# Linear attention into a SwiGLU block: k and v laid out with nine positions per partition and head pairs in two row halves, block 0's q with two tokens per partition, and one weight piece rounded earlier

## The chip, the cores and the metric

The kernel runs on one core of one Trainium2 chip. The metric is the device time of one execution in microseconds (us). Times in this document come from repeated executions and from one execution that was recorded by the hardware profiler; the profiled execution has its own time, which is given beside its span.

## What is computed

The reference is an attention without softmax, a norm, and then a gated feed-forward block, all in 32-bit floats:

```
q, k, v: (8 batches, 8 heads, 576 positions, 64)
kv  = einsum('bhsd,bhse->bhde', k, v)          # one 64x64 matrix per batch and head
out = einsum('bhsd,bhde->bhse', q, kv)
out = out / sqrt(mean(out*out, -1) + 1e-6) * g_norm
x   = out as (4608 tokens, 512)                # 8 heads x 64 side by side
y   = (silu(x @ w_gate) * (x @ w_val)) @ w_out # 512 -> 1536 -> 512
```

The weights are given as 64-bit floats. The kernel reads them as pairs of 32-bit words and rounds them to 32 bits itself.

## The kernel before, in words

**Blocks.** The 4608 tokens are cut into nine blocks of 512. A batch has 576 positions, so block n holds the end of batch n-1 and the start of batch n. `Att(n)` makes the normed attention output of block n, turned so that features lie on partitions (`self.x`), and `Ffn(n)` multiplies it with the weights. The attention of block n+1 is made inside the feed-forward work of block n. For block 0 nothing stands before it: `first` (L428) and `second` (L440) run at the start of the kernel.

**k and v.** `load_kv` (L215) loads, for a group g of four heads, two head pairs j = 2g and 2g+1. Of each pair, the lower 64 partitions hold the one part of the positions and the upper 64 the other: 5 positions per partition in one half and 4 in the other (5·64 + 4·64 = 576), so a load has runs of 1280 or 1024 bytes. That is four loads for k and four for v in each group, each onto 64 partitions. For block 0 v goes through ScalarE's queue (ACT's) and k through SyncE's (SP's). `kv` (L273) multiplies: each half of the rows accumulates into a PSUM tile of its own (`kv_ps[0]`, `kv_ps[1]`), ScalarE copies the first (L292), and VectorE adds the second to it (L293, helper line L111). Each of the 72 matmuls is 64x64: a quarter of the array[...].

**q.** `load_q` (L256) loads block 0's q as four loads of 128 tokens on 128 partitions, in runs of 64 values (256 bytes), and `turn_q` (L295) turns each 128 tokens by four 128x128 transposes on TensorE (L307), copied out by VectorE (the first) and ScalarE (the others). `product` (L313) multiplies with the 64x64 matrices, squares on ScalarE (L338) and sums on VectorE (L339). `root` (L341) finds 1/sqrt on VectorE in eleven small steps, `scale` (L359) applies it (helper line L113), `turn_x` (L366) turns the result on TensorE and multiplies by `g_norm` on ScalarE (L375).

**Weights.** `load_w` loads a piece of 512 KB (128 partitions, 1024-byte runs for gate and value pieces) into one of four `ld` buffers, which q also uses. `Words.round_to` (L138) rounds a piece: two ScalarE passes (L144 the low words, L146 the high words) and four on VectorE (L147, L152, L153, L157). The pieces go gate 0, value 0, gate 1, value 1 and so on; `plain_up` (L947) of output chunk f needs gate and value piece f.

**What orders the work.** The text is written in one order and a scheduler places each instruction on its engine's queue; each engine runs its queue in order. `tc.issue_after(x)` keeps what is inside it behind instruction x. Before the change the first two pieces (`weights(2)`) stand behind the squares and the scaling of block 0's first half. Loads take turns on a few semaphores, so an issue may also wait for an earlier load to land. In block 1's feed-forward, leaf weights for the later blocks are made on VectorE and stored to memory (`send`, L771); SP's queue holds these stores and the k and v loads of the next block in one line, and GpSimd (POOL) makes operand pieces (`t`, L112) in buffers that those stores have to release.

Of the kernel before, what the change touches and what calls it, by code (L numbers as in the profile page):

```python
# [8 lines left out]
F32 = mybir.dt.float32  # L9
# [5 lines left out]
P = 128  # L15
# [3 lines left out]
def kernel(  # L19
# [41 lines left out]
    nc = tc.nc  # L61
# [9 lines left out]
    NS = DM // P  # L71
    NF = FF // P
    NP = NF // 2
    KT = 5
    LD = 2 * (2 * KT - 1) * D
    eps = 1e-6
    assert NT == B * S and NT == NB * BLK and NB == B + 1 and S - BLK == BLK // B
    assert 2 * D == P and H == 2 * NS and (2 * KT - 1) * D == S and NS == 4

    def pool(name, bufs, **kw):  # L80
        return ctx.enter_context(tc.tile_pool(name=name, bufs=bufs, **kw))
# [37 lines left out]
    class Words:  # L119
# [18 lines left out]
        def round_to(self, dst):  # L138
            halves = self.raw.rearrange("p (f w) -> p f w", w=2)
            low, high = halves[:, :, 0], halves[:, :, 1]  # L140
            room = ring()

            unit = room[:, 0]
            nc.scalar.activation(out=unit, in_=low, func=ACT.Copy, scale=2.0**-51, bias=2.0)  # L144
            mag = room[:, 1].bitcast(U32)
            nc.scalar.activation(out=mag.bitcast(F32), in_=high.bitcast(F32), func=ACT.Abs)  # L146
            nc.vector.tensor_scalar(  # L147
                out=mag.bitcast(F32), in0=mag.bitcast(F32), scalar1=self.LOW, scalar2=self.HIGH,
                op0=OP.max, op1=OP.min,
            )  # L150
            sign = room[:, 2].bitcast(U32)
            nc.vector.tensor_scalar(out=sign, in0=high, scalar1=0x80000000, scalar2=None, op0=OP.bitwise_and)  # L152
            nc.vector.scalar_tensor_tensor(  # L153
                out=mag, in0=mag, scalar=3, in1=sign, op0=OP.logical_shift_left, op1=OP.bitwise_xor
            )
            a, b = self.shape[0], BLK // self.shape[0]
            nc.vector.tensor_tensor(  # L157
                out=dst.bitcast(U32),
                in0=mag.rearrange("p (a b) -> p a b", a=a, b=b),
                in1=unit.bitcast(U32).rearrange("p (a b) -> p a b", a=a, b=b),  # L160
                op=OP.add,
            )
# [22 lines left out]
    class Att:  # L185
# [28 lines left out]

        def load_kv(self, g):  # L215


            if self.n == B:
                return
            for i, (views, src) in enumerate(((self.k, k), (self.v, v))):  # L220
                tile_ = self.place_kv(g, i)
                for e in range(2):
                    j, s0 = 2 * g + e, 0
                    for r in range(2):
                        m = KT - (r != e)
                        at = 2 * D * (KT - r) * e
                        t = tile_[r * D : (r + 1) * D, at : at + 2 * D * m].rearrange("p (h x) -> p h x", h=2)
                        queue = nc.scalar if self.n == 0 and i else nc.sync
                        queue.dma_start(
                            out=t,  # L230
                            in_=src[self.n, 2 * j : 2 * j + 2, s0 : s0 + m * D].rearrange("h (p t) d -> p h (t d)", t=m),
                        )
                        views[j, r] = t.rearrange("p h (t d) -> p h t d", t=m)
                        s0 += m * D

        def load_quarters(self, i):

# [18 lines left out]
        def load_q(self, i):  # L256
            if self.n >= TURNED:
                self.load_quarters(i)
                return
            if self.n == 1:  # L260
                tiles = [t_tile().rearrange("p a b -> p (a b)") for _ in range(2)]
            else:
                ld = ld_pool.tile([P, LD], F32, name="ld")
                tiles = [ld[:, 0:BLK], ld[:, BLK : 2 * BLK]]
            for t in range(2):
                tile_ = tiles[t].rearrange("p (h d) -> p h d", h=H)
                for b, s0, p0, p1 in self.parts(2 * i + t):
                    nc.sync.dma_start(
                        out=tile_[p0:p1], in_=q[b, :, s0 : s0 + p1 - p0, :].rearrange("h p d -> p h d")
                    )  # L270
                self.q.append(tile_.rearrange("p (j u) d -> p j (u d)", u=2))

        def kv(self, g):  # L273


            if self.n == B:
                return
            if g == 0:
                self.kv_ps = [m_psum.tile([P, NS, D], F32, name="m") for _ in range(2)]
            for e in range(2):  # L280
                j = 2 * g + e
                for c in range(KT):
                    for r in range(2):
                        m = KT - (r != e)
                        for u in range(2 if c < m else 0):
                            nc.tensor.matmul(  # L286
                                self.kv_ps[r][u * D : (u + 1) * D, j, :], lhsT=self.k[j, r][:, u, c, :],
                                rhs=self.v[j, r][:, u, c, :], start=(c == 0), stop=(c == m - 1),
                            )
            if g == 1:  # L290
                dst = kvs[self.n % 3]
                nc.scalar.copy(out=dst, in_=self.kv_ps[0])  # L292
                self.kv_made = add(nc.vector, dst, self.kv_ps[1], dst)  # L293

        def turn_q(self, i, pools=None):  # L295

# [6 lines left out]
            for t in (2 * i, 2 * i + 1):  # L303
                pool = pools[t % 2] if pools else m_psum
                ps = pool.tile([P, NS, P], F32, name=pool.name[0])
                for j in range(NS):
                    nc.tensor.transpose(ps[:, j], self.q[t][:, j], ident)  # L307
                if t:
                    nc.scalar.copy(out=self.qt[:, t], in_=ps)
                else:  # L310
                    nc.vector.tensor_copy(out=self.qt[:, t], in_=ps)

        def product(self, i, pools=None):  # L313
# [7 lines left out]
            for t in range(2):  # L321
                for j in range(NS):
                    for b, _, p0, p1 in self.parts(2 * i + t):
                        for p in range(p0, p1, D):
                            for u in range(2):
                                rows = slice(u * D, (u + 1) * D)
                                nc.tensor.matmul(  # L327
                                    self.ps[i][u][p : p + D, t, j, :],
                                    lhsT=self.qt[rows, 2 * i + t, j, p : p + D], rhs=kvs[b % 3][rows, j, :],
                                    start=True, stop=True,  # L330
# [97 lines left out]
        def first(self):  # L428
            self.turn_q(0, (b_psum, c_psum))
            for g in range(2):  # L430
                self.kv(g)
            self.half(0)
            squared = self.squared
            self.turn_q(1, (b_psum, c_psum))
            with tc.issue_after(self.scaled.ins):
                self.product(1, (b_psum, a_psum))
            self.turn_x(0)
            return squared, self.scaled
# [437 lines left out]
    class Ffn:  # L876
# [3 lines left out]
            self.ps, self.making, self.leaf_room, self.ended = {}, [], None, None  # L880

        def store(self, o, t, columns=slice(None)):
            rows = out[BLK * self.n : BLK * (self.n + 1), columns].rearrange("(t p) d -> p t d", t=T)
            nc.sync.dma_start(out=rows[:, t : t + o.shape[1], :], in_=o)

        def h_sums(self, j, k, engine):

# [110 lines left out]
    blocks[0].load_q(0)  # L998
    for g in range(2):
        blocks[0].load_kv(g)  # L1000
    blocks[0].load_q(1)
    load_weights(4)
    squared, scaled = blocks[0].first()
# [89 lines left out]
```

## Time and profile before

| what | value |
|---|---|
| median of 5 runs | 1040.8 us (1039.66 to 1041.19) |
| profiled execution, its time | 1040.93 us |
| span of that execution in the trace | 1039.1 us, so 1.8 us lie around it |
| TensorE busy | 1009.7 us (97%) |
| VectorE, ScalarE, GpSimd busy | 700.3, 232.0, 368.9 us |
| mean granted TensorE clock | 0.997 |
| k loads in all (beside the start) | 26 of 160 KB and 26 of 128 KB, and as many for v |

The page gives the busy share of each engine, then the span in 40 slices, and then the chain of work that ended last: from the last instruction back to what released it, or to the instruction before it on its engine. A line of the chain, of the timeline and of a group names the source line (L286), the engine (PE is TensorE, PEld its weight loads, DVE VectorE, ACT ScalarE, SPq SyncE's queue) and the tile names, output first. "Issue" in the chain is time in which the engine waited for nothing that the profile shows. 32-bit matmuls appear as two records each, transposes as one.

### The profile page before, as it was taken

To read this page: it belongs to the slowest core of one execution; us is meant where nothing else is said; L and a number is where in the kernel's file an instruction comes from. 1 tells how busy PE (TensorE), PEld (TensorE's weight loads), DVE (VectorE), ACT (ScalarE), POOL (GpSimd) and SP (SyncE) were. 2 spreads that over 40 slices of the span, in tenths; PEclk is the share of its full clock that TensorE was granted. 3 is DMA by queue.
4 is the path that set the end of the run, shared out by engine and by line. 5 is a ranking of instruction groups with operands and counts; after the bars stand their busy time and mean duration, and the time that the engine had idled before them with its cause. 6 is when DMAs were issued, how large, how long until landed. Compare 5 with 4: busy or idle time off the path is not lost.

```text
span 1039.1 us, 21544 instructions
## 1 busy us (share of the span) xinstructions
PE 1009.7 (97%) x8588; PEld 906.2 (87%) x8588; DVE 700.3 (67%) x1202; ACT 232.0 (22%) x357; POOL 368.9 (35%) x280
## 2 busy tenths in 40 slices
PE   4899999899999999999999999999999999999998
PEld 3644688778899989998999899988999899989997
DVE  2999696788656866575666666684668566856661
ACT  3666111222212211211111111211122111212110
POOL 0000443435024621563147305640455136512670
PEclk9899999999999999999999999999999999999999
DMA  9588704765457556764676367736862666066611
GB/s 213 182 251 273 165 1 126 186 191 148 131 180 240 134 113 193 241 160 84 196 240 187 61 202 231 215 49 171 247 196 51 162 207 188 29 152 210 191 31 41
DMA packets 255044, 168.16 MB, mean 162 GB/s; under 512 B 124640, under 2 KB 230240, under 8 KB 254944
## 3 DMA queue, kind: packets, MB, share of 16 engines
q1 hardware_dynamic: 228384, 162.45, 55.8%
q10 hardware_dynamic: 26496, 4.33, 2.4%
q8 instruction: 68, 1.11, 0.4%
q14 instruction: 32, 0.26, 0.1%
q0 software_dynamic: 64, 0.00, 0.0%
HBM read 138.02 MB, written 22.41 MB: 154 GB/s over the span
## 4 chain that ended last, share of the span: by engine, by line
PE 89%; DVE 6%; DMA 3%; issue 1%; SPq 0%; POOL 0%; ACT 0%; DVEq 0%; POOLq 0%
PE b L662 25%; PE b L513 19%; PE c L662 12%; PE c L513 9%; PE a L662 6%; PE a L513 5%; PE b L956 4%; PE c L956 4%; PE m L286 1%; PE m L327 1%; DVE r L112 1%; DVE xi L112 1%; DVE r L111 1%; DMA h<-in_k_dram 1%; DVE t L111 1%
## 5 line engine op out<-in xcount | busy, mean ns | idle before, releaser
L111 POOL TENSOR_TENSOR r<-r 128x256 f32<-128x256 f32 (+1 forms) x105 | 110.8, 1061 | 309.1 <-DVE r L111 234.3
L111 DVE TENSOR_TENSOR r<-b,r 128x512 f32<-128x512 f32 (+1 forms) x273 | 162.0, 606 | 64.0 <-PE b L662 58.9
L112 POOL TENSOR_TENSOR t<-wo 128x512 f32<-128x512 f32 x81 | 115.3, 1447 | 195.5 <-DVE wo L111 107.8
L111 DVE TENSOR_TENSOR r<-c,r 128x512 f32<-128x512 f32 (+1 forms) x179 | 108.5, 618 | 89.1 <-PE c L662 49.5
L662 PE MATMUL b<-x,t 128*128 128x128 f32 x1092 | 151.0, 275 | 0.0
L662 PEld LDWEIGHTS b<-x,t 128*128 128x128 f32 x1092 | 136.5, 192 | 0.6
L111 DVE TENSOR_TENSOR r<-a,r 128x512 f32<-128x512 f32 (+1 forms) x99 | 62.5, 631 | 110.3 <-PE a L513 65.8
L113 POOL TENSOR_TENSOR h<-r 128x1024 f32<-128x1024 f32 (+1 forms) x40 | 81.6, 2057 | 87.3 <-DVE r L111 74.1
L662 PE MATMUL c<-xi,t 128*128 128x128 f32 x840 | 112.2, 275 | 0.3 <-DVE xi L111 0.3
L662 PEld LDWEIGHTS c<-xi,t 128*128 128x128 f32 x840 | 102.8, 192 | 0.4 <-DVE xi L111 0.4
L513 PE MATMUL b<-wo,h 128*128 128x256 f32 x432 | 99.4, 382 | 0.1
L513 PE MATMUL b<-t,h 128*128 128x256 f32 x432 | 96.9, 381 | 0.0
L513 PEld LDWEIGHTS b<-t,h 128*128 128x128 f32 x432 | 81.3, 190 | 11.3 <-issue 0.2
L513 PEld LDWEIGHTS b<-wo,h 128*128 128x128 f32 x432 | 79.9, 190 | 12.7 <-DVE h L113 2.5
L676 ACT COPY r<-b 128x512 f32<-128x512 f32 x63 | 36.9, 586 | 212.7 <-PE b L662 205.9
L662 PE MATMUL b<-xi,t 128*128 128x128 f32 x588 | 79.7, 276 | 0.0
L662 PEld LDWEIGHTS b<-xi,t 128*128 128x128 f32 x588 | 72.4, 192 | 0.0
L662 PE MATMUL b<-x,wg 128*128 128x128 f32 x336 | 52.7, 279 | 0.2 <-DVE x L112 0.2
L662 PE MATMUL b<-x,wv 128*128 128x128 f32 x336 | 51.3, 275 | 0.0
L956 PE MATMUL b<-x,wg 128*128 128x512 f32 (+1 forms) x112 | 45.8, 552 | 3.8 <-DVE wg L157 3.4
L513 PE MATMUL c<-t,s 128*128 128x256 f32 x216 | 48.3, 380 | 0.0
L513 PE MATMUL a<-wo,h 128*128 128x256 f32 x216 | 48.3, 379 | 0.0
(133 smaller groups left out, 1579.5 us busy)
## 6 DMA issues: line engine op xcount, KB each, us to landing
t<-w SPq DMA_DIRECT2D x336, 256.0 KB, 3.3
out_dram<-r SPq DMA_DIRECT2D x17, 512.0 KB, 3.1
ld<-in_moe_w_gate_dram SPq DMA_DIRECT2D x12, 512.0 KB, 4.6
ld<-in_moe_w_val_dram SPq DMA_DIRECT2D x12, 512.0 KB, 4.7
ld<-in_moe_w_out_dram SPq DMA_DIRECT2D x12, 512.0 KB, 5.1
w<-t SPq DMA_DIRECT2D x18, 256.0 KB, 2.5
w<-xi SPq DMA_DIRECT2D x12, 384.0 KB, 3.0
ld<-in_k_dram SPq DMA_DIRECT2D x26, 160.0 KB, 3.9
```

The source lines that it names most:

```text
L111: add = lambda e, o, a, b: e.tensor_tensor(out=o, in0=a, in1=b, op=OP.add)
L112: sub = lambda e, o, a, b: e.tensor_tensor(out=o, in0=a, in1=b, op=OP.subtract)
L113: mul = lambda e, o, a, b: e.tensor_tensor(out=o, in0=a, in1=b, op=OP.mult)
L286: nc.tensor.matmul(self.kv_ps[r][u * D : (u + 1) * D, j, :], lhsT=self.k[j, r][:, u, c, :], rhs=self.v[j, r][:, u, c, :], start=(c == 0), ...
L327: nc.tensor.matmul(self.ps[i][u][p : p + D, t, j, :], lhsT=self.qt[rows, 2 * i + t, j, p : p + D], rhs=kvs[b % 3][rows, j, :], start=True, ...
L513: nc.tensor.matmul(banks[e][:, e], lhsT=lhsT, rhs=rhs, start=first and i == 0 and (e == 0 or banks[0] is not banks[1]), stop=i == self.ste ...
L662: nc.tensor.matmul(ps[:, i, f], lhsT=self.weight(o, p, f), rhs=self.operand(o, p), start=first and (i, f) == (0, 0), stop=True, skip_group ...
L676: nc.scalar.copy(out=dst, in_=ps)
L956: nc.tensor.matmul(t, lhsT=w[f // 2][:, i, P * (f % 2) : P * (f % 2 + 1)], rhs=x[:, i, of], start=(i == 0), stop=(i == NS - 1),)
```

## The change

For every block, k and v are laid out with 9 positions per partition (`KT = 9`, runs of 2304 bytes): of the two head pairs in a group, the one lies wholly in the lower 64 partitions and the other wholly in the upper ones. A group then has two loads for k and two for v. k goes lower half first and v upper half first. No sum over the halves is left: each PSUM tile holds whole results for two head pairs, and is copied out by itself, in block 0 one on ScalarE and one on VectorE, in later blocks both on ScalarE.

Block 0's q is loaded as two loads of 256 tokens, two neighbouring tokens per partition (512-byte runs). It is turned by matmuls with the identity, one for each head (128 rows, 64 columns of the array) in place of transposes of head pairs: 16 matmuls for the 256 tokens where there were 8 transposes. Block 0's output rows are stored to fit.

The first gate piece is loaded between k's last load and q's second load, and is rounded behind the two copies of block 0's kv, ahead of the squares and sums of the first half. Turning q's second half now stands behind the product of the first half on TensorE. In rounding, ScalarE does the high words first.

```diff
-    KT = 5
-    LD = 2 * (2 * KT - 1) * D
+    KT = 9
+    LD = 2 * KT * D
...
             unit = room[:, 0]
-            nc.scalar.activation(out=unit, in_=low, func=ACT.Copy, scale=2.0**-51, bias=2.0)
             mag = room[:, 1].bitcast(U32)
             nc.scalar.activation(out=mag.bitcast(F32), in_=high.bitcast(F32), func=ACT.Abs)
+            nc.scalar.activation(out=unit, in_=low, func=ACT.Copy, scale=2.0**-51, bias=2.0)
...
                 tile_ = self.place_kv(g, i)
-                for e in range(2):
-                    j, s0 = 2 * g + e, 0
-                    for r in range(2):
-                        m = KT - (r != e)
-                        at = 2 * D * (KT - r) * e
-                        t = tile_[r * D : (r + 1) * D, at : at + 2 * D * m].rearrange("p (h x) -> p h x", h=2)
-                        queue = nc.scalar if self.n == 0 and i else nc.sync
-                        queue.dma_start(
-                            out=t,
-                            in_=src[self.n, 2 * j : 2 * j + 2, s0 : s0 + m * D].rearrange("h (p t) d -> p h (t d)", t=m),
-                        )
-                        views[j, r] = t.rearrange("p h (t d) -> p h t d", t=m)
-                        s0 += m * D
+                for r in (1, 0) if i else (0, 1):
+                    j = 2 * g + r
+                    t = tile_[r * D : (r + 1) * D].rearrange("p (h x) -> p h x", h=2)
+                    queue = nc.scalar if self.n == 0 and i else nc.sync
+                    queue.dma_start(
+                        out=t, in_=src[self.n, 2 * j : 2 * j + 2].rearrange("h (p t) d -> p h (t d)", t=KT)
+                    )
+                    views[j] = t.rearrange("p h (t d) -> p h t d", t=KT)
...
+            if self.n == 0:
+
+                ld = ld_pool.tile([P, LD], F32, name="ld")[:, 0 : 2 * BLK]
+                nc.sync.dma_start(
+                    out=ld.rearrange("p (h x) -> p h x", h=H),
+                    in_=q[0, :, HB * i : HB * (i + 1), :].rearrange("h (p t) d -> p h (t d)", t=2),
+                )
+                both = ld.rearrange("p (j u t d) -> p t j u d", j=NS, u=2, t=2)
+                self.q += [both[:, t] for t in range(2)]
+                return
...
-                self.kv_ps = [m_psum.tile([P, NS, D], F32, name="m") for _ in range(2)]
-            for e in range(2):
-                j = 2 * g + e
-                for c in range(KT):
-                    for r in range(2):
-                        m = KT - (r != e)
-                        for u in range(2 if c < m else 0):
-                            nc.tensor.matmul(
-                                self.kv_ps[r][u * D : (u + 1) * D, j, :], lhsT=self.k[j, r][:, u, c, :],
-                                rhs=self.v[j, r][:, u, c, :], start=(c == 0), stop=(c == m - 1),
-                            )
+                self.kv_ps = [m_psum.tile([P, 2, D], F32, name="m") for _ in range(2)]
+            for c in range(KT):
+                for r in range(2):
+                    k, v = self.k[2 * g + r], self.v[2 * g + r]
+                    for u in range(2):
+                        nc.tensor.matmul(
+                            self.kv_ps[r][u * D : (u + 1) * D, g, :], lhsT=k[:, u, c, :], rhs=v[:, u, c, :],
+                            start=(c == 0), stop=(c == KT - 1),
+                        )
             if g == 1:
-                dst = kvs[self.n % 3]
-                nc.scalar.copy(out=dst, in_=self.kv_ps[0])
-                self.kv_made = add(nc.vector, dst, self.kv_ps[1], dst)
+                dst = kvs[self.n % 3].rearrange("p (g r) d -> p r g d", r=2)
+                self.kv_made = [nc.scalar.copy(out=dst[:, 0], in_=self.kv_ps[0])]
+                if self.n:
+                    nc.scalar.copy(out=dst[:, 1], in_=self.kv_ps[1])
+                else:
+                    copied = nc.vector.tensor_copy(out=dst[:, 1], in_=self.kv_ps[1])
+                    self.kv_made.append(copied)
...
                 for j in range(NS):
-                    nc.tensor.transpose(ps[:, j], self.q[t][:, j], ident)
+                    if self.n:
+                        nc.tensor.transpose(ps[:, j], self.q[t][:, j], ident)
+                        continue
+                    for u in range(2):
+                        nc.tensor.matmul(ps[u * D : (u + 1) * D, j], lhsT=self.q[t][:, j, u], rhs=ident, start=True, stop=True)
...
-                                nc.tensor.matmul(
+                                self.multiplied = nc.tensor.matmul(
...
             for g in range(2):
                 self.kv(g)
+            with tc.issue_after(self.kv_made[0].ins), tc.issue_after(self.kv_made[1].ins):
+                weights(1)
             self.half(0)
             squared = self.squared
-            self.turn_q(1, (b_psum, c_psum))
+            with tc.issue_after(self.multiplied.ins):
+                self.turn_q(1, (b_psum, c_psum))
...
-            rows = out[BLK * self.n : BLK * (self.n + 1), columns].rearrange("(t p) d -> p t d", t=T)
-            nc.sync.dma_start(out=rows[:, t : t + o.shape[1], :], in_=o)
+            rows = out[BLK * self.n : BLK * (self.n + 1), columns]
+            if self.n:
+                rows = rows.rearrange("(t p) d -> p t d", t=T)[:, t : t + o.shape[1], :]
+            else:
+                rows = rows[P * t : P * t + HB].rearrange("(p t) d -> p t d", t=2)
+            nc.sync.dma_start(out=rows, in_=o)
...
     for g in range(2):
         blocks[0].load_kv(g)
+    load_weights(1)
     blocks[0].load_q(1)
```

## The prediction on record

> **What bounds the kernel now.** I read the page first, then the chain of waits by stretches, then the waits of TensorE, then the timelines of the stretches where the chain leaves TensorE. The page says that TensorE is nearly always busy:
>
> ```profile
> PE 1009.7 (97%) x8588; PEld 906.2 (87%) x8588; DVE 700.3 (67%) x1202; ACT 232.0 (22%) x357; POOL 368.9 (35%) x280
> ```
>
> So time can be won only where TensorE stands idle or runs slowly. From 245 us to the end its listed waits sum to 1.1 us, and between 40 and 245 us the only listed one is 6.6 us (4 times) for ScalarE's copies L563. The rest is the start. The chain there:
>
> ```profile
> 17.72 1.09 PE m L327 x63
> 18.80 0.94 issue
> ...
> 25.05 1.18 DVE z L339 x2
> ...
> 28.18 0.61 DVE wg L157
> 28.79 0.14 issue
> 28.93 3.75 PE b L956 x8
> 32.68 0.79 PE c L956 x4
> 33.47 1.17 issue
> 34.64 0.42 DVE h L113
> ...
> 37.01 0.61 DVE wg L157
> 37.62 0.04 issue
> 37.66 1.99 PE b L956 x8
> ```
>
> VectorE is to be seen as the limit from 20.67 to 28.79 and again from 34.64 to 37.62: norm of the first half, rounding of the first pieces, scaling of the second half, rounding of gate piece 1. From 37.66 to 116 us the chain is TensorE alone. I call T the end of kv (VectorE's L111, 17.15 + 0.42 = 17.57) and S the end of the first half's scaling (25.05).
>
> Stretches, with the TensorE clock as third figure from the right and GB/s as last:
>
> ```profile
> 5.00:7.90 2.90, 0.00 (x0) 0.00 (x0) 0.00 (x0) 0.00 (x0) 0.00 (x0) 1.00 1.10 228
> ...
> 18.00:21.00 3.00, 2.06 (x92) 1.69 (x84) 1.01 (x2) 1.90 (x4) 0.00 (x0) 1.00 1.09 345
> 25.10:28.90 3.80, 1.16 (x8) 0.86 (x9) 3.80 (x9) 3.29 (x7) 0.00 (x0) 0.62 0.17 50
> 28.90:33.50 4.60, 4.57 (x12) 3.77 (x13) 4.16 (x15) 2.08 (x3) 0.00 (x0) 0.57 0.60 187
> ```
>
> k and v move at 228 GB/s, weights at 345. And the first gate matmuls run at a clock of 0.57: eight records of 256 columns took 3.75 us there, 1.73 us at 43.97.
>
> Last, block 1's part, where SP's line holds k and v loads ahead of a store, and GpSimd waits for that store:
>
> ```profile
> 217.93 2.56 SPq L229 DMA_DIRECT2D ld<-in_k_dram  x4
> 220.53 0.60 SPq L229 DMA_DIRECT2D ld<-in_v_dram  x1
> 221.25 0.53 SPq L771 DMA_DIRECT2D w<-t  x1
> ```
> ```profile
> 224.45 1.26 POOL L112 TENSOR_TENSOR t<-wo 128x512 f32<-128x512 f32 x1 [3.08 <-DMA w<-t]
> ```
>
> [...] TensorE idle from 22 to 25.1, clock 0.62 and 0.57 after. [...] The trace has 64x64 tiles only: 140 records in 2.38 us, 17 ns each, though a record of 64 columns alone would take some 54 ns (a quarter of 1.73/8).
>
> **The change part by part.** Durations are from the profiled execution (1040.9 us, span 1039.1, 1.8 around it); it lies 0.1 above the median of 1040.8.
>
> *Loading.* q, k, v of block 0 up to the last k landing are 0.52 + 8·0.295 = 2.88 MB, landed at 16.02 (issue 11.62 + 4.4). Larger runs, eight issues instead of sixteen (0.6 us each). Estimate: q and the first v share a stretch at 290 GB/s (bounded by 228 and 345) from 2.1 to about 4.9 us. [...] I take 235 to 260. The first group is complete at about 11 [...], the last k at 13.5 to 14.4. First gain: 1.6 to 2.5 us of loading, before TensorE's part.
>
> *TensorE up to T.* Before, 8 transposes took 12.06 to 13.95, 236 ns each, twice the 110 ns at 119.5: the clock was half there too. Now 16 matmuls of two records, 128 columns each, so 32·108 ns = 3.5 us one after the other at full clock (1.73/16 = 108), 1.7 if the two column halves run together; 3.5 and 6.9 at half clock. I take 3.5, half clock and together. From 11.0: 18 kv matmuls, 36 records at 34 = 1.2; q 3.5; the other 54 kv, 108 records at 17 to 20 = 2.0; sum 17.7. The two copies now run beside each other: 0.35 instead of 0.37 + 0.42. T = 18.1, 0.5 later than before; bounds 16.5 and 20.5. So loading's gain is eaten by q's turn. The wait for q's second load (17.02) that stood ahead of the product goes, but kv was due at 17.57 anyway: nothing.
>
> *T to S.* Product, square, sums, root, scale: unchanged, 7.48, including the 0.94 of issue, which I keep. New in it: VectorE rounds gate piece 0 (L152 0.34, L147 0.34, L153 0.60, L157 0.61 = 1.9) ahead of the first sum, which before began at T + 1.92 with VectorE idle. ScalarE's two passes (1.1 us) precede the squares, in the 1.3 us of product. Piece 0 must have landed by T: it follows the last k in SP's line, 0.52 MB at 345 is 1.5, so 15 to 16.5. Rounding ends at T + 2.3, the first sum moves 0.4, but the second sum, late by the issue gap before (20.67), absorbs it: nothing. If piece 0 lands after T, ScalarE's squares and VectorE's sums queue behind it and S moves one for one. In SP's line q's second load and value piece 0 come behind piece 0. Queued behind the wait for q are its turning, product 1 and turn_x: at 290 GB/s it lands about 1.8 after piece 0, near 18, and is wanted at T + 2.2, so it holds nothing; value piece 0, 1.5 later, is wanted at S + 1.5. Turning q's second half (1.7 to 3.5) and its copies now stand between the products: product 1 ends at T + 5.7 to 7.4, its squares by T + 8.6, against sums at T + 7.5: nothing to 0.5.
>
> *S to gate piece 1.* Before: 37.62 - 25.05 = 12.57. Now VectorE: two sums 1.2, value piece 0 with two root steps mixed in to 3.4, the rest of the root 1.9, scale 0.6 to 5.9, h 0.35, scale 0.6 to 6.9, gate piece 1 2.6: 9.5. That is 3.1 less: 1.9 of rounding and the 1.17 stall. It holds if TensorE's first gate matmuls run at full clock: x is ready at S + 2.1, gate 1.73, value 1.73, end S + 5.6, before h at 5.9. I expect it: the 32 extra records and the later product shrink the idle stretch to 1 or 2 us. At half clock, 5.6 us from S + 2.1 end at 7.7 and piece 1 comes at 11.3: 1.3 less.
>
> *Block 1's part.* Three k and v issues instead of five stand ahead of the store at 221.25: 2·0.63 = 1.25 us sooner. Its data are ready at 218.3, so the store really moves. GpSimd's t, its h and VectorE's h L112 (idle 2.46) follow, and TensorE's wait of 1.80 at 230.32 shrinks; the VectorE chain from there carries it on past the next wait at 241.55. I take 1.2, bounds 0 and 1.6. The add (0.34) leaving VectorE at 217.4 is hidden behind SP's line.
>
> *Elsewhere.* kv's 72 matmuls, later copies, stores: beside a TensorE without waits, nothing. If that cover fails, two ScalarE copies cost under 0.8 us a block.
>
> Sum: +0.5 - 3.1 - 1.2 = -3.8; 1040.9 - 3.8 = 1037.1.
>
> **Rivals.** *Half clock stays:* idle between the first half's parts still trips it. For: 0.57 before; against: more work in the gaps. +0.5 - 1.3 - 1.2 = -2.0: 1038.9. *Halves pair well:* [...] first group at 9.6, T 16.6: -1.0 - 3.1 - 1.2 = -5.3: 1035.6. [...] *Slower:* q's turning on 64 columns does not overlap and the clock stays half through it: 1.2 + 6.9 + 108·34 ns = 3.7 from 11 gives 22.8, T = 23.2, 5.6 late; -1.3 - 1.2 follows: +3.1, 1044.0. It decides from T of about 20.1 on (with half clock) or 21.9. For: no trace row shows two column halves alone; against: 64x64 tiles overlap threefold. *Nothing at block 1 and a late piece 0:* near 1040.5.
>
> **How the numbers follow.** Forecast 0.45, half clock 0.20, good pairing 0.17, slower 0.13, nothing 0.05. 0.2% (2.1 us, threshold 1038.7) is about what a measurement can tell from no change. Faster: nearly all of the first, the third, a fifth of the second: 0.64; slower 0.14; within 0.22. Range 1034.8 to 1041.3: below, good pairing (1035.6) with block 1 at 1.6 and the issue gap gone (the second sum some 0.4 sooner); above, T at its bound of 20.5 (+2.9) with half clock (-1.3) and block 1 (-1.2), +0.4. It leaves out the slower case and little more.
>
> **What would show it.** k and v GB/s above 228 before 13 us; T near 18; the rounding of gate piece 0 inside T to T + 2.4 with sums on time; the first gate matmuls at about 1.73 us and no issue stall before h; the first store behind k and v in block 1 about 1.25 us sooner and TensorE's waits there near 5.4. Wrong if q's turn takes over 5 us, if piece 0 lands after T, or if TensorE waits anew past 40 us.

## The result, and the profile after

The changed kernel took 1042.93 us (median of 23 runs, 1040.18 to 1044.86) against 1040.80 us for the kernel before on the same chip (43 runs): ratio 1.0021, 95% interval 1.0015 to 1.0026. It became slower by 0.2%, about 2 us. The forecast was 1037.1 us and faster; the result lies 1.6 us above the end of its range.

The profiled execution took 1040.18 us (span 1038.4, again 1.8 around it) and is the shortest of all its runs; the median is 2.75 us longer. A second sample of the same kernel, the run "after again", left a trace of an execution of 1043.74 us (span 1042.0): 0.8 above that median, and the longest of the 13 in its own sample, whose median is 1041.7. So the one trace stands at the lower end of the spread, the other in its upper half. Both are used below, and the difference between them is part of the answer.

The page hardly tells the two kernels apart:

```profile
PE 1009.9 (97%) x8636; PEld 906.5 (87%) x8636; DVE 700.4 (67%) x1195; ACT 232.4 (22%) x364; POOL 368.8 (36%) x280
```

TensorE has 48 records more (a record is one matmul entry of the trace, with its weight load) and 0.2 us more busy time. The chain of waits at the start does tell them apart. Columns: start, length, what.

```profile
1.52 8.89 DMA h<-in_v_dram
...
10.54 2.53 PE m L288 x40
13.07 1.90 PE b L317 x16
14.97 1.71 PE c L317 x16
16.68 2.06 PE m L288 x96
...
19.09 1.02 PE m L337 x43
20.10 2.27 issue
22.38 0.52 PE m L337 x15
...
27.24 1.29 DVE r L113 x2
```

Before, loads ended the waits up to 17.06 us. Here TensorE itself is the limit from 10.54 on: 40 kv records (matmuls of k with v), 32 records for q's first half, the other kv records. Product 0 starts at 19.09 instead of 17.65, and inside it, where 0.94 us of issue stood before, stand 2.27. The first half is scaled (S, the end of L113) at 28.53 instead of 25.05.

In the stretches, k and v move no faster. Columns as in the prediction: the TensorE clock, the DMA share and GB/s are the last three.

```profile
5.00:7.90 2.90, 0.00 (x0) 0.00 (x0) 0.00 (x0) 0.00 (x0) 0.00 (x0) 1.00 1.04 207
7.90:10.50 2.60, 0.00 (x0) 0.00 (x0) 0.00 (x0) 0.00 (x0) 0.00 (x0) 1.00 1.05 222
10.50:13.00 2.50, 2.46 (x40) 2.37 (x41) 0.00 (x0) 0.00 (x0) 0.00 (x0) 1.00 1.06 242
```

207 and 222 GB/s stand against 228 in both stretches before, and 242 against 236 in the third. The last k landed at 15.85 us (15.99 in "after again"), against 16.06 before.

### The profile page after: what moved, and what is told of

Read it like the earlier page. It is cut to its first block, busy times and chain, and to the rows that moved or that the text cites. A ratio compares the mean times of both kernels' runs of the same rounds, so it can differ in the third digit from the quotient of the medians.

```text
span 1038.4 us, 21562 instructions
## 1 busy us (share of the span) xinstructions
PE 1009.9 (97%) x8636; PEld 906.5 (87%) x8636; DVE 700.4 (67%) x1195; ACT 232.4 (22%) x364; POOL 368.8 (36%) x280
## 4 chain that ended last, share of the span: by engine, by line
PE 89%; DVE 6%; DMA 2%; issue 1%; ACT 0%; POOL 0%; SPq 0%; ACTq 0%; DVEq 0%; POOLq 0%
PE b L675 25%; PE b L526 19%; PE c L675 12%; PE c L526 9%; PE a L675 6%; PE a L526 5%; PE b L973 4%; PE c L973 4%; PE m L288 2%; PE m L337 1%; DVE xi L112 1%; DVE r L112 1%; DMA h<-in_v_dram 1%; DMA w<-t 1%; DVE t L111 1%
## 5 line engine op out<-in xcount | busy, mean ns | idle before, releaser
L113 POOL TENSOR_TENSOR h<-r 128x1024 f32<-128x1024 f32 (+1 forms) x40 | 81.5, 2051 | 88.5 <-DVE r L111 75.9
L526 PEld LDWEIGHTS b<-t,h 128*128 128x128 f32 x432 | 81.3, 190 | 11.3 <-issue 0.2
L526 PE MATMUL c<-wo,h 128*128 128x256 f32 x216 | 48.1, 379 | 0.0
```

Source lines behind the costliest of these rows:

```text
L113: mul = lambda e, o, a, b: e.tensor_tensor(out=o, in0=a, in1=b, op=OP.mult)
L526: nc.tensor.matmul(banks[e][:, e], lhsT=lhsT, rhs=rhs, start=first and i == 0 and (e == 0 or banks[0] is not banks[1]), stop=i == self.ste ...
```

## How two executions of the changed kernel differ

The first eight records of gate product 0 (256 columns each), in the profiled execution and in "after again":

```profile
30.02 1.99 PE L973 MATMUL b<-x,wg 128*128 128x256 f32 x8 [0.34 <-ACT x L385]
```
```profile
30.64 3.78 PE L973 MATMUL b<-x,wg 128*128 128x256 f32 x8
```

1.99 us against 3.78: in the second trace the granted clock is 0.50 from 28.02 to 34.85 us, in the first it is 1.00 from 17.2 us almost to the end. Spells of half clock lasted 6.83 us in the trace of the kernel before (26.01 to 32.83) and in "after again", and 3.41 us in that of "q first, kept busy" (20.06 to 23.47, below); they begin at other times in each execution. The idle stretch ahead of this stage does not decide it alone: TensorE waited 2.36 us for the first half's scaling (L113) in both traces of the changed kernel, and met the half clock behind it in one of them only.

The mean clock listed with each run falls with the spells (0.997 for the kernel before, with its one of 6.83 us inside the span), but it does not order the times by itself. Of the 13 runs of "after again", the one at 1.000 took 1040.1 us, four at 0.998 took 1041.1 in the mean, three at 0.997 took 1041.8, five at 0.995 took 1042.4. Of the 24 executions listed with the result, two at 1.000 took 1040.2 us, but seven at 0.998 took 1042.7, one of five at 0.997 took 1040.3 and six at 0.995 took 1043.2. And of the five runs of "q as before" (below), the three at 0.995 are the fastest. The mean doesn't say where a spell fell ("q as before" has one at 199.4 to 202.8 us, far from the start), and something else adds to it.

One such thing shows in "after again": a wait of 2.41 us in block 1, ahead of the products that turn a part of q, where the profiled execution goes on at once. The first line is of "after again", the second of the profiled execution:

```profile
124.28 0.66 PE L314 MATMUL c<-ident,t 128*128 128x128 f32 x4 [2.41 <-DVE r L321]
```
```profile
119.84 0.66 PE L314 MATMUL c<-ident,t 128*128 128x128 f32 x4
```

The view puts the wait down to VectorE's copy L321. But that copy had ended 0.7 us earlier, and in the profiled execution the same products start 0.9 us before that copy does. Block 1's q loads weren't late either: the last of them landed at 119.15. What these products have in common with the gap in product 0 is told below, under "What the issue gap is".

## The experiments

Each row is one trace; the last column is from all runs of that kernel. "Product 0" is where it starts (T in the prediction, within 0.1), "gap" the longest issue wait of TensorE before S (idle time for which the trace shows no cause), S the end of the first half's scaling (L113), "gate 1" the start of gate piece 1's matmuls. Times in us.

| run | product 0 | gap, and where | S | first gate b x8 | gate 1 | span | median, ratio to before [95%] |
|---|---|---|---|---|---|---|---|
| before | 17.65 | 0.94, end of product 0 | 25.05 | 3.75 | 37.66 | 1039.1 | 1040.8 |
| after | 19.09 | 2.27, product 0 | 28.53 | 1.99 | 38.02 | 1038.4 | 1042.93, 1.0021 [1.0015, 1.0026] |
| after again | 19.45 | 2.07, product 0 | 28.69 | 3.78 | 40.14 | 1042.0 | 1041.7, 1.0009 [1.0001, 1.0017] |
| q as before | 17.47 | 2.09, behind product 0 | 25.09 | 2.80 | 35.28 | 1035.2 | 1037.04, 0.9969 [0.9956, 0.9981] |
| q first | 18.08 | 0.40, product 0 | 26.67 | 1.99 | 36.99 | 1037.8 | 1038.84, 0.9986 [0.9979, 0.9992] |
| round late | 19.63 | 1.70, product 0 | 28.50 | 3.75 | 42.57 | 1045.0 | 1046.48, 1.0054 [1.0041, 1.0066] |
| round alone | 17.20 | 2.39, behind product 0 | 24.50 | 1.99 | 34.48 | 1035.7 | 1038.22, 0.9975 [0.9964, 0.9986] |
| kv alone | 17.65 | 1.58, behind product 0 | 24.98 | 3.75 | 38.53 | 1038.9 | 1041.76, 1.0013 [1.0004, 1.0022] |
| q first, kept busy | 17.80 | 1.76, product 0 | 27.24 | 1.99 | 36.73 | 1039.5 | 1039.63, 0.9988 [0.9981, 0.9994] |
| idle records early | 23.64 | 2.07, in kv | 31.07 | 3.30 | 41.30 | 1041.2 | 1043.01, 1.0019 [1.001, 1.0028] |
| fewer kv records | 17.97 | 2.62, behind product 0 | 25.43 | 1.99 | 37.42 | 1037.3 | 1038.39, 0.9977 [0.997, 0.9984] |
| gap put back | 18.94 | 1.66, product 0 | 27.75 | 2.67 | 37.80 | 1038.7 | 1039.74, 0.9991 [0.9984, 0.9997] |
| kept busy | 17.29 | 2.06, behind product 0 | 24.75 | 1.99 | 34.70 | 1034.2 | 1037.5, 0.9967 [0.9954, 0.9979] |

### Which part costs: the first four runs

**After again**: the changed kernel, no edit.

> The changed kernel once more, for a second trace: the recorded execution of it took 1040.2 us, the median of all is 1042.9, so the trace that exists is of an early one. Theory A (the start decides): the median execution loses its 2 to 3 us before 40 us, by a TensorE clock that falls to half between product and the first gate matmuls, and the first gate matmul of piece 1 starts near 40 us instead of 38.0; from there on the time to the end is that of the recorded one within 0.5 us. Theory B (the later blocks decide): the start is as recorded (38.0 us) and the 2 to 3 us appear after 40 us, as waits of TensorE for streamed tiles or for block 1's leaf weights.

1041.7 us; its trace is read above. Both theories hold in part: gate piece 1 starts 2.1 us later than in the profiled execution, almost all of it behind S, where the clock is at half (0.50 from 28.02 to 34.85); and another 1.4 us go after that, where the wait of 2.41 us stands.

**q as before**: block 0's q is loaded, turned and stored as in the kernel before; k, v and the early rounding stay changed.

```diff
-            if self.n == 0:
-                ld = ld_pool.tile([P, LD], F32, name="ld")[:, 0 : 2 * BLK]
...
-                    for u in range(2):
-                        nc.tensor.matmul(ps[u * D : (u + 1) * D, j], lhsT=self.q[t][:, j, u], rhs=ident, start=True, stop=True)
+                    nc.tensor.transpose(ps[:, j], self.q[t][:, j], ident)
```

> Only block 0's q (loads of 256-byte runs, transposes, store) is put back to the form before; all else is the changed kernel. Theory A, with q's turning as ordinary matmuls at half clock as its largest part: kv is made 1.5 to 2 us sooner than the 19.05 of the changed kernel, the whole is 1.5 to 2.5 us faster than the changed kernel, near 1040.8. Theory C (q's form is harmless since the loads of k and v bound the start): within 0.5 us of the changed kernel.

1037.04 us, faster than both kernels, and 3.8 below the 1040.8 that was expected. So the whole loss sits in block 0's q, with two tokens per partition; the run puts its load, its turning and its store back together and doesn't tell them apart. Against "after again" the trace is 6.8 us shorter: 2.0 up to product 0, 1.6 from there to S, 1.3 from S to gate piece 1, and 1.9 after it. Product 0 starts at 17.47, and the issue gap has moved:

```profile
17.47 1.26 PE L323 MATMUL m<-kv,r 64*64 64x64 f32 x64 [0.28 <-ACT kv L284]
18.70 0.65 PE L303 MATMUL b<-ident,ld 128*128 128x128 f32 x4
21.45 0.64 PE L303 MATMUL c<-ident,ld 128*128 128x128 f32 x4 [2.09 <-issue]
```

It is as long as in the changed kernel, but it falls between the two parts of q's second half, which nothing waits for before S.

**q first**: in the changed kernel, q's first half is turned ahead of all kv products, while TensorE waits for k and v.

```diff
-            for g in range(2):
-                self.kv(g)
+            with tc.issue_after(self.turned_q.ins):
+                for g in range(2):
+                    self.kv(g)
```

> The changed kernel with one order turned: on TensorE, q's first half is turned ahead of all kv matmuls, while k and v are still loading. Theory A: the 3.6 us of turning leave the path between the first and the last kv matmul, kv is made at about 16 us instead of 19.05, and the whole is about 3 us faster than the changed kernel, near 1040. Theory B: no change beyond 0.5 us in the median, since what is lost is lost later. If the loads bound the start, kv is made at 17.5 or later.

1038.84, lower than the 1040 expected, though kv isn't made near 16 us: its last 72 records wait for v until 15.32. Product 0 starts 1.0 us sooner (18.08 for 19.09) and the gap is 0.40. But the trace shows the full clock only from 25.59 on, and product 0's two parts take 1.75 and 0.91 us instead of 1.02 and 0.56.

**Round late**: the changed kernel without the early rounding of gate piece 0.

```diff
-            with tc.issue_after(self.kv_made[0].ins), tc.issue_after(self.kv_made[1].ins):
-                weights(1)
```

> The changed kernel with gate piece 0 rounded where it was before (behind the scaling of the first half). Theory A: VectorE gets 1.9 us more between scaling and gate piece 1; 1 to 2 us slower than the changed kernel, near 1044.5. Theory D (the early rounding is what hurts, since it holds up ScalarE's squares and VectorE's sums): faster than the changed kernel by 1 us or more.

1046.48, where 1044.5 was expected: the early rounding is worth 3.6 to 4.8 us in the changed kernel (from 1042.93 and 1041.7). S is as late as with it (28.50); gate 1 starts 14.07 after S instead of 9.49 to 11.45.

### Each part on the kernel before

**Round alone**: gate piece 0 loaded ahead of q's second half and rounded ahead of the norm, with what belongs to it in the change: q's second half turned behind product 0, and ScalarE's two rounding passes in the other order (not in the lines shown). k, v, block 0's q and the stores are as before.

```diff
+            with tc.issue_after(self.kv_made.ins):
+                weights(1)
...
+            with tc.issue_after(self.multiplied.ins):
+                self.turn_q(1, (b_psum, c_psum))
...
+    load_weights(1)
     blocks[0].load_q(1)
```

> The kernel before with one part of the change alone: gate piece 0 is loaded ahead of q's second half and rounded ahead of the norm, and q's second half is turned behind the first product. k, v, q and the stores stay as before. Theory A (the early rounding carries the whole gain of the variant with q as before, 1037.0, and k and v by nine positions carry next to nothing): T near 17.6, S near 25.1, gate piece 1 at S + 9.5 to 11.4, time 1037.0 to 1038.0. Rival B (the layout of k and v brings about half of it, at the start or by the sooner stores in block 1): about 1039. Rival C (piece 0 on the queue ahead of q's second half costs the start): S later than 26, 1040 or more.

1038.22: this part alone takes 2.7 us off, at the upper edge of what was expected. In the trace the gain lies between S and gate piece 1: 9.98 us, where it was 12.61. Part of that may be the clock, since the first gate products took 1.99 us in this trace and 3.75 before. Turning q's second half behind product 0 also takes four records out of product 0's way, and the gap now falls among these four:

```profile
17.20 1.16 PE L327 MATMUL m<-kv,r 64*64 64x64 f32 x64 [0.82 <-DVE kv L111]
18.29 0.55 PE L307 MATMUL b<-ident,ld 128*128 128x128 f32 x3
21.23 0.33 PE L307 MATMUL b<-ident,ld 128*128 128x128 f32 x1 [2.39 <-issue]
```

**kv alone**: k and v with nine positions, head pairs in upper and lower rows; the rest as before.

```diff
-    KT = 5
+    KT = 9
...
+                for r in (1, 0) if i else (0, 1):
+                    j = 2 * g + r
+                    t = tile_[r * D : (r + 1) * D].rearrange("p (h x) -> p h x", h=2)
```

> The kernel before with k and v by nine positions and head pairs in upper and lower rows alone; q, the order of loads and the rounding stay as before. Theory A: T stays at 17.5 since kv waits for its last load then too, S at 25.0, block 1's stores come 0.5 to 1 us sooner: time 1039.8 to 1040.6, no change that can be told. Rival B: 1038.5 to 1039 (half of the 3.8 us). If it is slower than before, 64-row loads of larger runs cost something that the rounding hides.

1041.76, ratio 1.0013 [1.0004, 1.0022]: no gain, if anything a small loss, where 1039.8 to 1040.6 was expected. Product 0 starts at 17.65 as before.

### The half clock, and what it uncovers

**q first, kept busy**: q first, with 5 and 6 idle products of 128 columns ahead of the two groups of kv.

```diff
+            for g, count in enumerate((5, 6)):
+                with tc.issue_after(after.ins):
+                    for i in range(count):
+                        warmed = nc.tensor.matmul(warm[:, 0:P], lhsT=ident, rhs=ident, start=True, stop=True)
+                with tc.issue_after(warmed.ins):
+                    self.kv(g)
+                after = self.made
```

> The changed kernel with q's first half turned ahead of all kv products, and with 5 and 6 idle products of 128 columns (into a product bank that is free then) ahead of the first and of the second 36 kv products, so that TensorE has no gap of over 1 us from 6 us to T. Theory A (the clock at half carries the loss left in the q-first variant): clock at full from 13 us at the latest, kv's last 72 records 1.3 us instead of 2.4, T 17.0 instead of 18.1, product 0 at 1.0 us plus the issue gap instead of 3.06 in all, q's second half 1.9 instead of 3.6; S 25.0 to 25.7, time 1036.5 to 1037.5 against 1038.8. Rival F (the issue gap is bound to an instruction block that arrives at its own time, and a faster TensorE only reaches the gap sooner): the gap grows from 0.40 to 1.5 to 2.0 and falls at record 22 of product 0, S near 26, time about 1038.

1039.63, not faster than q first without them, and above what either theory expected. The clock is at full from 9.81 to 20.06 and the last kv records take 1.27 us instead of 2.58, but product 0 starts only 0.28 sooner, since the last k lands at 16.25. Then the gap comes, after 22 records, as the rival expected:

```profile
17.80 0.67 PE L337 MATMUL m<-kv,r 64*64 64x64 f32 x22 [0.28 <-ACT kv L294]
20.23 1.44 PE L337 MATMUL m<-kv,r 64*64 64x64 f32 x42 [1.76 <-issue]
```

Both here and in q first, product 0 goes on at 20.23. A faster TensorE reached the gap sooner and waited longer. The clock then was at half again from 20.06 to 23.47, and S came at 27.24, later than in q first (26.67).

**Kept busy**: q as before, with 5 idle products of 128 columns behind product 1.

```diff
+            with tc.issue_after(self.multiplied.ins):
+                for i in range(5):
+                    warmed = nc.tensor.matmul(warm[:, 0:P], lhsT=ident, rhs=ident, start=True, stop=True)
```

> The variant with block 0's q as before (1037.0), with 5 idle products of 128 columns behind product 1, in the 1.13 us that TensorE waits for the scaling there. Theory A (half clock over the first gate products costs that variant 0.8 to 2 us in the executions that have it): TensorE's clock falls to half less often or for a shorter time, time 1036.0 to 1036.8. Rival: [...] five idle products do not tip it: 1037.0, and where the clock is at half they delay the turning of x by 0.1 to 0.3: up to 1037.4.

1037.5 against 1037.04: no difference that can be told, as the rival expected. This trace ran the first gate products at full clock and has the shortest span of all, but "round alone" ran them at full clock too, without idle products.

### What the issue gap is

In every trace but the two with idle records at the very start ("idle records early" and "gap put back"), the gap stands before TensorE's 220th or 221st matmul record, counted from the start of the kernel, whatever that record does.

**Idle records early**: the changed kernel, same order, with 112 idle products of 32 columns ahead of everything.

```diff
+            for i in range(112):
+                rows = slice(D * (i % 2), D * (i % 2) + D)
+                last = nc.tensor.matmul(idle[rows, 0:32], lhsT=ident[0:D, 0:D], rhs=ident[0:D, 0:32], start=True, stop=True)
```

> The changed kernel, order unchanged, with 112 idle products of 32 columns (224 matmul records) on TensorE ahead of everything, in the time in which it waits for q, k and v. In six traces the issue gap falls at TensorE's 220th matmul record, whatever that record belongs to. Theory F (the gap is the arrival of the next instruction block): no gap in product 0; it falls behind the idle products, before 10.5 us, where TensorE waits for k and v anyway; S - T shrinks from 9.4 to about 7.5, time 1040.3 to 1041.0 if nothing else moves (2 us less than the changed kernel), unless the block after it comes due inside kv or product 0. Rival G (the gap belongs to product 0, to its memory or to a wait that the trace does not show): still 2 us at record 44 of product 0, time as the changed kernel's, 1041.7 to 1042.9.

1043.01, where 1040.3 to 1041.0 was expected. Two misses: the idle records took 54 ns each, 12.15 us in all, more than TensorE had to spare, so kv started at 15.21; and the next gap came too.

```profile
2.43 12.15 PE L444 MATMUL a<-ident 64*64 64x32 f32 x223 [2.43 <-POOL ident masks.py:199]
15.08 0.21 PE L444 MATMUL a<-ident 64*64 64x32 f32 x1 [0.50 <-issue]
15.21 1.46 PE L288 MATMUL m<-h 64*64 64x64 f32 x40
...
19.24 1.03 PE L288 MATMUL m<-h 64*64 64x64 f32 x53
22.34 1.03 PE L288 MATMUL m<-h 64*64 64x64 f32 x51 [2.07 <-issue]
23.64 1.26 PE L339 MATMUL m<-kv,r 64*64 64x64 f32 x64 [0.27 <-ACT kv L296]
```

The gaps stand after 223 records and after 223 + 1 + 40 + 32 + 53 = 349, 126 later. Product 0 has none, and S - T is 31.07 - 23.64 = 7.43, as expected. So the gap goes with the count of records and not with product 0.

The count goes on. The products behind the wait of 2.41 us in "after again" begin with TensorE's 729th record, 508 behind the 221st, which is four times 127. All four traces with the changed kernel's number of records have TensorE idle there: 0.04 us in the profiled execution, 2.41 in "after again", and, with no releaser at all, 0.45 in "q first" and 0.80 in "round late" (one line of each):

```profile
120.19 0.66 PE L314 MATMUL c<-ident,t 128*128 128x128 f32 x4 [0.45 <-issue]
```
```profile
125.09 0.63 PE L314 MATMUL c<-ident,t 128*128 128x128 f32 x4 [0.80 <-issue]
```

In the trace's DMA records a 16 KB packet of an instruction queue lands 1.2 to 1.6 us before each of these gaps ends: here at 13.52 and 20.93, gaps ending at 15.08 and 22.34; in the kernel before at 18.23 and 19.74; in the changed kernel at 21.05 and 22.38, and at 118.40 ahead of its 729th record at 119.84; in "after again" at 122.89 and 124.28. The number of packets goes with the count of records too: the profiles count 68 of them with 8588 TensorE records, 69 with 8636 and 70 with 8860, and at the step measured, 127 records to a packet, these records would need 67.6, 68.0 and 69.8. So TensorE seems to have waited for its next instructions; that is inferred from the count and the times, since no view names it as the releaser. TensorE stood still for up to 2.6 us (2.62 in "fewer kv records", below).

**Fewer kv records**: the changed kernel with 12 of block 0's 72 kv products left out, 24 records fewer ahead of product 0.

```diff
-            for c in range(KT):
+            steps = KT - 3 if self.n == 0 and g == 0 else KT
+            for c in range(steps):
...
```

> The changed kernel with 12 of block 0's 72 kv products left out (the last three of nine steps of the first two head pairs), so 24 matmul records fewer ahead of product 0; part of the kv sum is left out. In all earlier traces the issue gap falls at TensorE's 220th record, and with 224 more records it came 128 records later too, inside kv. Theory F: the gap now falls at what would be record 68 of product 0's 64, so behind it; product 0 runs in 1.2 us without a gap, T is 0.2 to 0.5 us sooner for the missing products, S - T is 7.5 (VectorE's rounding then ends last) against 9.2 to 9.5: S at 26.3 to 26.8 against 28.5 to 28.7, time 1040.0 to 1041.0, about 2 us below the changed kernel. If the gap belongs to product 0, it stays at its record 44 with 2 us, and the time falls by 0.2 to 0.5 only.

1038.39, 3.3 to 4.5 us below the two samples of the changed kernel; 2 were expected.

```profile
17.97 1.26 PE L338 MATMUL m<-kv,r 64*64 64x64 f32 x64 [0.28 <-ACT kv L295]
19.16 0.44 PE L318 MATMUL b<-ident,ld 128*64 128x128 f32 x4
22.22 1.24 PE L318 MATMUL b<-ident,ld 128*64 128x128 f32 x12 [2.62 <-issue]
```

The gap is behind product 0 by four records, as counted, though q is still turned in the new form. S - T is 7.46, as expected; product 0 starts 1.1 us sooner, where 0.2 to 0.5 were expected. The 12 products left out are worth some 0.4 of that, an estimate from 24 records at 17 ns; the clock was at full from 15.77 (17.18 in the changed kernel), and whether that is chance or comes from the edit was not tried. So not all of the gain is the gap's.

**Gap put back**: q as before, with 24 idle records at 3 us, and kv's first 36 products ahead of q's turning.

```diff
+            for i in range(12):
+                rows = slice(D * (i % 2), D * (i % 2) + D)
+                last = nc.tensor.matmul(idle[rows, 0:32], lhsT=ident[0:D, 0:D], rhs=ident[0:D, 0:32], start=True, stop=True)
+            with tc.issue_after(last.ins):
+                self.kv(0)
```

> The variant with block 0's q as before (1037.0), with 12 idle products of 32 columns (24 records, 1.3 us) at 3 us, where TensorE waits for loads until 10.4; the first 36 kv products stand together ahead of q's turning. Theory F: T stays at 17.4 to 17.8; the gap moves from behind product 0 to its record 44 to 48 and takes 1.5 to 2.3 us there; S - T grows from 7.56 to 9.0 to 9.5, S at 26.7 to 27.2, time 1038.5 to 1039.5, 1.5 to 2 us above that variant. This would give the share of the gap in the 5.9 us between that variant and the changed kernel. If 24 idle records leave S at 25.1, the gap is not what costs.

1039.74, 2.7 us above the variant without the idle records and 0.2 above the range expected.

```profile
18.94 0.99 PE L323 MATMUL m<-kv,r 64*64 64x64 f32 x45 [0.36 <-ACT kv L284]
21.60 0.56 PE L323 MATMUL m<-kv,r 64*64 64x64 f32 x19 [1.66 <-issue]
```

The gap is back inside product 0, behind 45 of its 64 records, and S - T grows from 7.62 to 8.81. The other half of the loss is an accident of the edit: with kv's first group whole ahead of q, TensorE waits for k until 13.21, and product 0 starts 1.5 later.

## Why the prediction was wrong, point by point

The sum is set against "after again", since the profiled execution is the shortest. Predicted span: 1037.1 - 1.8 = 1035.3. Measured: 1042.0, so 6.7 too long.

| term | before | predicted | after again | difference from predicted | profiled execution |
|---|---|---|---|---|---|
| T | 17.65 | 18.1 | 19.45 | +1.35 | 19.09 |
| T to S | 7.40 | 7.48 | 9.24 | +1.76 | 9.44 |
| S to gate piece 1 | 12.61 | 9.5 | 11.45 | +1.95 | 9.49 |
| gate piece 1 to the end | 1001.4 | 1001.4 - 1.2 = 1000.2 | 1001.8 | +1.6 | 1000.4 |

**T (+0.5 predicted, +1.4 to 1.8 measured).** The price of q's turning was right: 1.90 + 1.71 = 3.6 us for 16 matmuls against 3.5, with the column halves running together: q's second half, as many records, took 1.9 us at a recorded clock of 1.00, where 3.5 was estimated for one after the other. That the clock was at half for the first half is read from the times alone, 3.6 against 1.9, since this trace's clock records begin at 17.18 us (the views show 1.00 ahead of that). Wrong was the kv term: 36 records at 34 ns, 1.2 us, were counted ahead of q; 40 records took 2.53 us, 63 ns each. The 34 ns was scaled from a stretch in which the records of both row halves stood in turn (17 ns each); here one head pair's k and v are there at 10.4, the other pair's last k only at 11.85 (the whole group was predicted for 11.0), and the first 24 records, all of one pair, took 1.3 us, 54 ns each. After q, 104 records took 2.1 us, as predicted (2.0). With q as before the same kv waits only for its last load and T is 17.47; so 1.6 to 2.0 us of T is q's form. The bound of 20.5 held.

**T to S ("unchanged, 7.48, including the 0.94 us of issue, which I keep").** This is the step that failed most instructively. The gap wasn't a constant of product 0. It goes with TensorE's 220th or 221st record. The 24 extra records that turn q's first half on 64 columns (32 for 8), less the four that turned a part of q's second half ahead of product 0 before, moved it from ahead of the last record of product 0 to behind the 44th of 64, where both sums wait for it, and it grew to 2.1 to 2.3 us. The prediction also let the rounding hide in the same stretch, and that was right: with no gap in product 0, S - T is 7.3 to 7.6 in five variants, rounding and all.

**S to gate piece 1 (9.5, or 11.3 at half clock).** Both figures were right: 9.49 at full clock, 11.45 at half. The choice between them was the error. It isn't one or the other for all executions: the same kernel gave 9.49 in one trace and 11.45 in another, and of the 24 executions listed with the result, 22 have a mean clock below 1.000 (0.995 to 0.998). The rival "half clock stays" deserved more than 0.20.

**Gate piece 1 to the end (-1.2).** The store in block 1 moved as predicted: it stood 3.32 us behind the first k issue (217.93 to 221.25), and stands 2.01 behind it now (218.30 to 220.31). But GpSimd then takes an h ahead of its t, and by the starts of its matmuls TensorE gains only 0.7 us there (0.39 behind the kernel before at 205 to 215 us, 0.32 ahead at 243 to 260) and 0.9 in "after again". The whole term came to -1.0 in the profiled execution, near the forecast. In "after again" the wait of 2.41 us ahead of the 729th record more than takes it back; by the count of records it belongs with the gap in product 0. The prediction had put "elsewhere" at nothing, and had named a new wait of TensorE past 40 us as a sign of being wrong.

**Loading.** The estimate of 235 to 260 GB/s was too high: 207 to 242. The last k was forecast for 13.5 to 14.4 and landed at 15.85, against 16.06 before, so the 1.6 to 2.5 us of loading that q's turning was to eat up were not there. Larger runs and fewer issues brought no time that shows, and the layout alone (kv alone) gave nothing at the start.

**The rivals.** The slower case (1044.0) named q's turning without overlap as its mechanism. The time came out near it by luck, for other reasons: the overlap was there (1.9 us for the 32 records of q's second half at a clock of 1.00, where 3.5 was estimated without it). None of the rivals counted instruction records.

What stays open: what sets off the next 16 KB packet. Without the early idle records it starts anywhere from 16.9 to 20.0 us, and not at a fixed record, so the length of the gap couldn't be foretold from the profile before. The pause ahead of the 729th record was read from traces and not tried alone; how often it is long, and how much of the spread from 1040 to 1045 us comes from it or from the half clock, isn't known. Nor is the difference between 1041.7 and 1042.93 us for the same kernel in two sets of runs resolved.

The best version measured is the change without its part for block 0's q: 1037.04 us, ratio 0.9969 [0.9956, 0.9981]. The early rounding with its order of work alone gives 0.9975 [0.9964, 0.9986]; the intervals overlap, so no gain of the k and v layout is shown beside it.

## What to carry to other kernels

An issue gap in a chain of waits need not be a fixed cost of the line it stands on. Count the engine's records from the start in several traces: if gaps stand at a fixed count, and further ones whole steps of some 127 records on (as here, at 221 and 729), an edit that adds records ahead moves them, and they may land on the critical path. Not every step shows a gap, so look too at waits whose named releaser had long been done. When a stage depends on the TensorE clock after an idle stretch, forecast a mixture of the full and the half clock (here 1.99 or 3.78 us for the same eight records), and place the profiled execution among all the runs before taking it as typical.

## What was not expected of the hardware

- A TensorE issue gap of 0.4 to 2.6 us before matmul record 220 to 224, once again 126 records later, and of up to 2.4 us 508 records later, ending 1.2 to 1.6 us after a 16 KB instruction packet landed, while loads were running.
- 64x64 records that write to two row halves of the result in turn took 54 ns each whether they had 32 columns (12.15 us for 223 idle records) or 64 (1.3 us for the first 24 kv records), both ahead of 15.1 us. Narrower records brought nothing there, which is why the idle records were too slow.
- Matmuls of 128 columns on two 64-column halves of the array ran at the same time, by their times: 32 records took 1.9 us at a clock of 1.00 (q's second half in the profiled execution, 22.87 to 24.8), where the prediction's estimate for one after the other is 3.5, from 108 ns a record. As many took 3.6 us from 13.07 on (q's first half), ahead of that trace's first clock record.
